# The second batch takes its keys and queries as runs of four tokens and turns them on TensorE

## The chip, the cores and the metric

The kernel is one program on one core of one Trainium2 chip. The metric is the device time of one execution in microseconds (us). Five engines work side by side, each on its own list of instructions and in the order of that list: TensorE (PE: matmuls and transposes; PEld is its weight load), VectorE (DVE), ScalarE (ACT), GpSimd (POOL) and SyncE (SP, which here only issues DMAs). They meet through semaphores. Matmul results land in PSUM, which has eight banks here; everything else lives in SBUF.

## The reference

```python
def _attn_ref(q, k, v, p):                 # q, k, v: (8, 8, 576, 64); p: (8, 8, 32, 64)
    p_packed = sm_attn(p, k, v)            # 32 packed rows read 576 keys
    out = sm_attn(q, p_packed, p_packed)   # 576 queries read the 32 packed rows
    # sm_attn: softmax(q k^T / sqrt(64)) v, the maximum taken away, 1e-9 added to the sum
def _moe_ref(x, w_in, w_out, a, b):        # x: the attention's 4608 x 512, heads side by side
    h = x @ w_in                           # 512 -> 2048
    P = a[0] + a[1]*h + a[2]*h**2 + a[3]*h**3
    Q = 1 + abs(b[0])*abs(h) + abs(b[1])*h**2
    return ((P / (Q + 1e-6)) @ w_out)      # 2048 -> 512
```

The two weight matrices come in 64-bit floats and everything else in 32-bit ones. The kernel computes `h` and the last product to float32 accuracy from three products of 32-bit halves (high by high, low by high, high by low).

## The kernel before

**Batches and units.** The work runs over 8 batches. For each batch `attention(bb)` makes the softmax weights over the 32 packed rows for all heads (tiles `AH` and `AL`, high and low half) and the transposed packed values `PPT`. The second attention product is never formed alone: `m_chunk` multiplies the packed values with a piece of `w_in` (256 of its 2048 columns, one chunk) into the tiles `m`, and a *unit* then goes from `AH`/`AL` and `m` to `h` (`hidden`: PE, tile `h`), through the rational function (ACT and DVE, tiles `Y`, `U`, `V`, `sq`) and on to the output sums (`acc_block`: PE, tile `acc`, from `gh`/`gl` and the split `w_out` pieces in `w`). There are 128 units: 8 batches x 2 halves of the tokens x 8 chunks. Units 0 to 15 are the first batch; a chunk of `m` is made ahead of the unit that first reads it.

**The weights.** `w_in` and `w_out` come in 16 pieces of 1 MB (64-bit words), each as two DMAs of 512 KB, first into the `m` tiles and then into the `w` tiles and `o`. `convert()` turns one piece into 32-bit floats with two ACT and three DVE instructions (`TENSOR_SCALAR`, `SCALAR_TENSOR_TENSOR` and one that the profile calls `CUSTOM_DVE_ANT_0` and the listings below `ISA`); a `w_out` piece is then split by ACT and POOL. All 16 conversions lie among the first dozen units.

**Keys and queries.** `load` fetches what a batch needs, `transposed` in `attention` brings keys and queries into the tile `kx` with the head dimension on partitions. There are two ways:

- First batch (`bb == 0`): a DMA gives each of 128 partitions four tokens in a row, 1 KB from one place. For 2 heads x 2 halves PE transposes 128x128 blocks, four into one PSUM bank, and ACT copies the bank to `kx` (128x512). The 64 tokens beyond 512 are loaded apart into `r`, transposed apart and copied apart (`krem` for the keys, two small copies for the queries). In this form the two halves of the tokens get softmax maxima of their own, and the factors `f`, `fs`, `F` join them.
- All other batches: four DMAs per group of four heads fetch 32-element rows (128 bytes) so that one DVE block transpose of 32x32 blocks, 128x576 at a time, writes `kx` directly. A batch takes four such transposes for its keys and four for its queries.

A batch's keys are loaded, and its remainders and `p`, while the batch before is in `attention`; its values after its keys are transposed, its queries after its values are used, since all share the two `nat` buffers. The second batch's attention runs as 16 steps among units 1 to 14 of the first.

**PSUM.** `bank(bb)` hands out the banks: the first batch takes turns on `acc` and `at` (four banks), the others on `at` alone (two banks), which `m_chunk` uses too.

**What sets the order.** Nothing runs as the code is written. `Planner` records every instruction, prices it from a table (`COST`, `TRANSPOSE`; a DMA by the length of its runs, `DMA_RATE`: 100, 190 or 370 bytes per ns for runs under 256 bytes, under 1 KB, and longer), builds the dependencies, schedules them in a list on the five engines, and issues each engine's instructions in that order. So another price or another instruction moves things everywhere. All instructions carry line 216, the planner's issue; one goes by the tiles' names.

Of the kernel before, what the change touches and what calls it, by code (L numbers as in the profile page):

```python
# [13 lines left out]
F32 = mybir.dt.float32  # L14
# [9 lines left out]
P = 128  # L24
# [7 lines left out]
class Planner:  # L32
# [8 lines left out]
    TRANSPOSE, F32 = (15, 0.834), (30, 1.667)  # L41
# [206 lines left out]
def attention_rational_ffn(  # L248
# [15 lines left out]
    NG = 2  # L264
# [160 lines left out]

    NAT, AH, AL, PPT = {}, {}, {}, {}

    def load(bb, what):  # L430
        if bb >= B:
            return
        if what == "rem":

            rv, pn = NAT[bb, "rv"], NAT[bb, "p"] = rv_ring.next(), pn_ring.next()
            if bb == 0:
                r = NAT[bb, "r"] = Y_ring.at(2, [P, H, D])
                nc.sync.dma_start(r[0:REM], k[bb, :, NS * P : T, :].rearrange("h p d -> p h d"))
            for j in range(NJ):
                src = p[bb, NG * j : NG * j + NG].rearrange("r n d -> n r d")  # L440
                nc.sync.dma_start(pn[32 * j : 32 * j + 32, :, 0, :], src)
            nc.gpsimd.tensor_copy(pn[:, :, 1, :], pn[:, :, 0, :])
            for i in range(2 if bb == 0 else 0):
                src = q[bb, 4 * i : 4 * i + 4, NS * P : T, :].rearrange("h (p x) d -> p h (x d)", x=2)
                r2 = r[REM + HREM * i : REM + HREM * (i + 1)].rearrange("p (h x) d -> p h (x d)", x=2)
                nc.sync.dma_start(r2, src)
            for i in range(2):
                src = v[bb, 4 * i : 4 * i + 4, NS * P : T, :]
                if bb == 0:
                    nc.sync.dma_start(rv[REM * i : REM * (i + 1)], src.rearrange("h p d -> p h d"))  # L450
                    continue
                for y in range(2):
                    o = REM * i + HREM * y
                    nc.sync.dma_start(rv[o : o + HREM], src.rearrange("h (p y) d -> y p h d", y=2)[y])
            return
        x, g = what[0], int(what[1])
        src = {"k": k, "q": q, "v": v}[x][bb, 4 * g : 4 * g + 4]
        if bb > 0:
            t = NAT[bb, what] = nat_ring.next()
            if x == "v":  # L460
                t = NAT[bb, what] = t[:, 0 : 4 * NS * D].rearrange("p (h s d) -> p h s d", h=4, s=NS)
                for y in range(2):
                    to = t.rearrange("p h (y i) d -> p h y (i d)", y=2)[:, :, y]
                    nc.sync.dma_start(to, src[:, 2 * P * y : 2 * P * (y + 1)].rearrange("h (p i) d -> p h (i d)", i=2))
                return
            src = src.rearrange("h t d -> (h t) d")
            for i in range(2):
                for y in range(2):
                    o = 64 * i + 32 * y
                    blocks = src[:, 32 * y : 32 * y + 32].rearrange("(a t i) d -> i t a d", t=32, i=2)[i]  # L470
                    nc.sync.dma_start(t[o : o + 32].rearrange("p (a d) -> p a d", d=32), blocks)
            return
        src = src[:, 0 : NS * P, :]
        if x != "k":
            if g == 0:
                NAT[x] = w_ring.at(NCH - 2 + "vq".index(x), [P, 2, 4 * NS * D], F32)
            t = NAT[x][:, g, :]
        else:
            t = nat_ring.next()[:, 0 : 4 * NS * D]
        t = t.rearrange("p (h s d) -> p h s d", h=4, s=NS)  # L480
        nc.sync.dma_start(t, src.rearrange("h (p s) d -> p h s d", s=NS))
        NAT[bb, what] = t
# [18 lines left out]
    def attention(bb):  # L501
# [7 lines left out]
        xr = lambda x: x.rearrange("p (x r) -> p x r", r=NG)  # L509
        eng = nc.vector if bb == 0 else nc.gpsimd  # L510
        KX = kx_ring.next()
        AH[bb], AL[bb], PPT[bb] = AH_ring.next(), AL_ring.next(), ppT_ring.next()
        flat = KX.rearrange("p j c -> p (j c)")
        rows = lambda i: slice(64 * i, 64 * i + 64)
        cols = lambda j: slice(32 * j, 32 * j + 32)
# [4 lines left out]
        qx = flat.rearrange("p (r j c) -> p r j c", r=NG, j=NJ)  # L520

        def transposed(x, g):
            for r in range(NG if bb > 0 else 0):

                src = NAT[bb, f"{x}{g}"].rearrange("p (j r c) -> p r j c", j=2, r=NG)[:, r]
                nc.vector.transpose(qx[:, r, 2 * g : 2 * g + 2, :], src)
            for r in range(NG if bb == 0 else 0):
                t = bank(bb)
                for i in range(2):
                    for y in range(2):  # L530
                        o = (2 * i + y) * P
                        nc.tensor.transpose(t[:, o : o + P], NAT[bb, f"{x}{g}"][:, 2 * i + r, 2 * y : 2 * y + 2, :], ident)
                to = kmain if x == "k" else qx[:, :, :, 0:HMAIN]
                nc.scalar.copy(to[:, r, 2 * g : 2 * g + 2, :], t.rearrange("p (j c) -> p j c", j=2))
# [4 lines left out]
                load(bb, f"v{g}")  # L539
            yield  # L540
        rkq = NAT.get((bb, "r"))
        if bb == 0:
            t = bank(bb)
            for j in range(NJ):
                nc.tensor.transpose(t[:, j * P : (j + 1) * P], rkq[:, 2 * j : 2 * j + 2, :], ident)
            nc.scalar.copy(krem, t.rearrange("p (j c) -> p j c", j=NJ)[:, :, 0:REM])
# [3 lines left out]
        nc.scalar.copy(pT, t[:, 0 : NG * P].rearrange("p (r c) -> p r c", r=NG))  # L550
        yield

        KEYS = ((0, 2 * P), (2 * P, T)) if bb == 0 else ((0, HALF), (HALF, T))
        of = lambda a, r: a.rearrange("p (x r) -> p x r", r=NG)[:, :, r]
        for r in range(NG):
            t = [bank(bb)[:, 0 : c1 - c0] for c0, c1 in KEYS]
            if bb > 0:

                for b in (slice(0, 2 * P), slice(2 * P, HALF)):
                    tiles(  # L560
                        (
                            (t[x][cols(j), o], pT[rows(x), r, cols(j)], qx[rows(x), r, j, b]),
                            dict(start=True, stop=True),
                        )
                        for j in range(NJ)
                        for x, o in ((0, b), (1, slice((b.start + HREM) % HALF, (b.stop + HREM - 1) % HALF + 1)))
                    )
                for x in range(2):
                    nc.vector.reduce_max(mx[:, 2 * x + r : 2 * x + r + 1], t[x], axis=AX.X)
                bias = nbm[:, r : r + 1]  # L570
                nc.vector.tensor_scalar(bias, mx[:, r : r + 1], mx[:, 2 + r : 3 + r], -SCALE, ALU.max, ALU.mult)
                for x, (c0, c1) in enumerate(KEYS):
                    i = slice(2 * x + r, 2 * x + r + 1)
                    nc.scalar.activation(KX[:, r, c0:c1], t[x], AF.Exp, bias=bias, scale=SCALE, accum_out=sm[:, i])
                if r == 0:
                    yield
                continue
# [19 lines left out]
                nc.scalar.activation(KX[:, r, c0:c1], t[x], AF.Exp, bias=nb[:, i], scale=SCALE, accum_out=sm[:, i])  # L597
            if r == 0:
                yield
        if bb == 0:  # L600
            nc.vector.tensor_tensor(nbm, nb[:, 0:2], nb[:, 2:4], ALU.min)
            nc.vector.tensor_sub(xr(f), two(nbm), xr(nb))
            nc.scalar.activation(f, f, AF.Exp)
            nc.vector.tensor_mul(fs, f, sm)
        else:
            fs = sm
        nc.vector.scalar_tensor_tensor(tot, fs[:, 0:2], 1e-9, fs[:, 2:4], ALU.add, ALU.add)
        nc.vector.reciprocal(rec, tot)
        if bb == 0:
            nc.vector.tensor_mul(xr(F), xr(f), two(rec))  # L610
        yield

        for r in range(NG):
            t = bank(bb)
            for s in range(NS):
                c0 = s * P + (REM if bb > 0 and s > 1 else 0)
                nc.tensor.transpose(t[:, s * P : (s + 1) * P], KX[:, r, c0 : c0 + P], ident)
            nc.scalar.copy(KX[:, 2 + r, 0 : NS * P], t)
            if r == 1:

                t = bank(bb)
                for i in range(NG):
                    o = slice(i * P, (i + 1) * P)
                    if bb > 0:
                        nc.tensor.transpose(t[:, o], KX[:, i, HALF + HREM - P : HALF + HREM], ident)
                        nc.tensor.transpose(t[0:REM, o], KX[:, i, 2 * P : 2 * P + REM], ident)
                        continue
# [4 lines left out]

        t = bank(bb)
        rv = NAT[bb, "rv"]
        for r in range(NG if bb > 0 else 0):
            tiles(
                (
                    (
# [10 lines left out]
                for s in range(NS + 1)  # L649
                for j in range(NJ)  # L650
            )
        for r in range(NG if bb == 0 else 0):
            for x, blocks in enumerate((range(2), range(2, NS + 1))):
                o = slice((2 * r + x) * D, (2 * r + x + 1) * D)
                tiles(
# [19 lines left out]
        twice = lambda o: o.rearrange("p (i d) -> p i d", i=1).broadcast_to([P, 2, D])  # L675
        for r in range(NG):
            o = pp[:, r]
            if bb > 0:
                nc.vector.tensor_scalar(o, twice(t[:, r * D : (r + 1) * D]), rec[:, r : r + 1], None, ALU.mult)
            else:  # L680
                nc.vector.tensor_scalar(o, twice(t[:, 2 * r * D : (2 * r + 1) * D]), F[:, r : r + 1], None, ALU.mult)
# [6 lines left out]
        for g in range(2):  # L688
            transposed("q", g)
            load(bb + 1, f"k{g}")  # L690
            if g == 0 and bb == 0:
                t = bank(bb)
                for j in range(NJ):
                    nc.tensor.transpose(t[:, j * P : (j + 1) * P], rkq[:, 2 * j : 2 * j + 2, :], ident)
# [4 lines left out]
                load(bb + 1, "rem")  # L699
            yield  # L700

        for r in range(NG):
            t = [bank(bb)[:, 0:HALF] for _ in range(2)]
            tiles(
# [135 lines left out]
    def acc_block(u, i):  # L840
# [10 lines left out]
        if i == 0:  # L851
            O[bb, x] = o_ring.next()
        o = O[bb, x]
        order = "(p i x) m -> p x i m" if bb == 0 else "(i p x) m -> p x i m"
        ov = out[bb * T : bb * T + NS * P, :].rearrange(order, i=2, x=2)[:, x]
        if u == NU - 1 and i == 1:
            nc.vector.tensor_copy(o[:, i, :], acc)
# [95 lines left out]
```

## Time and profile before

| what | value |
| --- | --- |
| median of 3 runs | 809.83 us (808.62 to 809.86) |
| the profiled execution | 808.45 us, of which the span from the first to the last instruction is 806.7 us |
| busy share of the span | PE 92%, PEld 73%, DVE 88%, ACT 83%, POOL 58% |
| mean granted TensorE clock | 0.958 |
| moved by DMA | 56.04 MB in 168,876 packets, 140,384 of them under 512 bytes |
| all weights converted | at 145.75 us, the end of the last `CUSTOM_DVE_ANT_0` |
| first output store issued | at 153.81 us (units 0 to 7 are through) |

The chain that ended last has PE for 70% of the span, DVE 10%, ACT 8%, SP's queue 4% and DMA 4%. Busy shares are means over the whole span. The stretch before some 150 us, in which weights arrive and are converted, has other limits than the rest, and it is read by itself. A group's row gives count, busy time, mean ns of one, and then the idle time before them. Rows of one engine overlap by their ends, so the step from one start to the next is shorter than the duration.

### The profile page before, as it was taken

What the parts mean: (1) busy time and instruction counts of PE and PEld (TensorE: products, weight loads), DVE (VectorE), ACT (ScalarE), POOL (GpSimd) and SP (SyncE); (2) the same over time, 40 slices, a digit from 0 to 9 for tenths busy, and PEclk for the clock granted to TensorE, in tenths of its full rate; (3) what the DMA queues carried; (4) which work ended last, traced back from release to release, by engine and by line L of the source; (5) the groups of instructions that cost most, each with busy time, mean ns of one, the idle gap of its engine ahead of it and who ended that gap; (6) DMA issues with size and microseconds to landing.
All of it is one profiled execution on the core that took longest, in us unless ns stands there. A gap on an engine that the chain in (4) does not pass through costs nothing.

```text
span 806.7 us, 15198 instructions
## 1 busy us (share of the span) xinstructions
PE 745.5 (92%) x5416; PEld 585.4 (73%) x5416; DVE 709.1 (88%) x1310; ACT 666.0 (83%) x1482; POOL 463.9 (58%) x462
## 2 busy tenths in 40 slices
PE   6376686899999999999999999999999999999997
PEld 4154464578877788768878788678877887778886
DVE  2988999898899788998899789998899789998873
ACT  4788797799888798889888798889888788998972
POOL 0003564675568455766578555756568456766663
PEclk9765799799999999999999999999999999999999
DMA  8993238202550206220730209120820214000001
GB/s 267 280 298 110 105 78 110 43 5 79 67 86 1 79 18 96 56 57 28 94 58 1 82 15 119 33 56 27 103 49 5 75 33 67 1 2 27 27 1 39
DMA packets 168876, 56.04 MB, mean 69 GB/s; under 512 B 140384, under 2 KB 158048, under 8 KB 168800
## 3 DMA queue, kind: packets, MB, share of 16 engines
q1 hardware_dynamic: 168800, 55.07, 31.4%
q8 instruction: 42, 0.69, 0.4%
q14 instruction: 34, 0.28, 0.1%
HBM read 45.62 MB, written 9.44 MB: 68 GB/s over the span
## 4 chain that ended last, share of the span: by engine, by line
PE 70%; DVE 10%; ACT 8%; SPq 4%; DMA 4%; issue 2%; POOL 1%; DVEq 0%; POOLq 0%
PE acc L216 35%; PE h L216 22%; PE at L216 13%; DVE Y L216 5%; SPq L216 4%; ACT Y L216 2%; DVE w L216 1%; ACT U L216 1%; ACT V L216 1%; ACT w L216 1%; DMA w<-in_q_dram 1%; ACT sq L216 1%; DVE V L216 1%; POOL w L216 1%; DVE kx L216 1%
## 5 line engine op out<-in xcount | busy, mean ns | idle before, releaser
L216 PE MATMUL acc<-w,gh 128*128 128x512 f32 x1024 | 330.5, 405 | 19.3 <-ACT w L216 15.0
L216 PEld LDWEIGHTS acc<-w,gh 128*128 128x128 f32 x1024 | 186.7, 191 | 72.7 <-ACT w L216 16.6
L216 POOL TENSOR_TENSOR U<-U,sq 128x576 f32<-128x576 f32 x118 | 168.9, 1432 | 75.4 <-ACT U L216 43.3
L216 PE MATMUL h<-AH,m 128*128 128x288 f32 x1024 | 192.0, 309 | 8.8 <-DVE Y L216 6.1
L216 POOL TENSOR_TENSOR gl<-Y,gh 128x512 fp32r<-128x512 f32 x128 | 167.7, 1310 | 50.5 <-ACT gh L216 23.3
L216 PE MATMUL acc<-w,gl 128*128 128x512 f32 x512 | 193.2, 398 | 0.3 <-POOL gl L216 0.3
L216 PEld LDWEIGHTS h<-AH,m 128*128 128x128 f32 x1024 | 162.7, 195 | 40.5 <-DVE Y L216 23.1
L216 ACT ACTIVATE Y<-h,abS 128x288 f32<-128x288 f32 x256 | 125.2, 509 | 23.5 <-PE h L216 19.3
L216 DVE TENSOR_TENSOR Y<-Y,h 128x288 f32<-128x288 f32 x256 | 109.9, 446 | 32.0 <-ACT Y L216 12.0
L216 ACT ACTIVATE sq<-h 128x288 f32<-128x288 f32 x236 | 97.5, 416 | 40.2 <-PE h L216 34.1
L216 DVE SCALAR_TENSOR_TENSOR Y<-Y,abS,h 128x288 f32<-128x288 f32 x256 | 125.5, 508 | 2.2
L216 DVE SCALAR_TENSOR_TENSOR Y<-Y,abS,V 128x576 f32<-128x576 f32 x128 | 103.4, 808 | 22.7 <-ACT V L216 22.0
L216 PEld LDWEIGHTS acc<-w,gl 128*128 128x128 f32 x512 | 96.8, 189 | 28.0 <-issue 8.5
L216 PE MATMUL h<-AL,m 128*128 128x288 f32 x512 | 113.0, 302 | 0.0
L216 POOL COPY G<-Y 128x64 f32<-128x64 f32 x128 | 35.5, 277 | 125.8 <-DVE Y L216 109.1
L216 ACT ACTIVATE U<-h 128x288 f32<-128x288 f32 x256 | 98.1, 421 | 8.7 <-PE h L216 4.3
L216 ACT ACTIVATE V<-U,one 128x576 f32<-128x576 f32 x128 | 98.0, 766 | 5.8 <-DVE Y L216 5.6
L216 DVE SCALAR_TENSOR_TENSOR Y<-V,Y 128x576 f32<-128x576 f32 x128 | 95.8, 749 | 1.8
L216 DVE SCALAR_TENSOR_TENSOR V<-U,V 128x576 f32<-128x576 f32 x128 | 96.4, 753 | 0.0
L216 ACT CAST gh<-Y 128x512 fp32r<-128x512 f32 x128 | 81.2, 634 | 7.4 <-DVE Y L216 7.0
L216 PEld LDWEIGHTS h<-AL,m 128*128 128x128 f32 x512 | 85.1, 194 | 0.9 <-issue 0.8
L216 ACT ACTIVATE V<-V 128x576 f32<-128x576 f32 x128 | 84.6, 661 | 0.6
(123 smaller groups left out, 813.2 us busy)
## 6 DMA issues: line engine op xcount, KB each, us to landing
nat<-in_k_dram SPq DMA_DIRECT2D x56, 144.0 KB, 4.1
nat<-in_q_dram SPq DMA_DIRECT2D x56, 144.0 KB, 4.2
out_dram<-o SPq DMA_DIRECT2D x15, 512.0 KB, 2.9
w<-in_moe_w_out_dram SPq DMA_DIRECT2D x14, 512.0 KB, 5.0
nat<-in_v_dram SPq DMA_DIRECT2D x28, 256.0 KB, 3.6
m<-in_moe_w_in_dram SPq DMA_DIRECT2D x8, 512.0 KB, 9.6
w<-in_moe_w_in_dram SPq DMA_DIRECT2D x8, 512.0 KB, 5.5
nat<-in_k_dram SPq DMA_DIRECT2D x2, 512.0 KB, 4.8
```

Source lines behind the costliest of these rows:

```text
L216: getattr(getattr(self.nc, engine), name)(*args, **kwargs)
```

## The change

`rows4(bb)` replaces `bb == 0` wherever the form of the loads is chosen, and is true for the first two batches. The second batch then loads keys, queries and values as 1 KB runs, PE transposes keys and queries and ACT copies them, its remainder goes through `r`, and its softmax joins two halves by factors. Its output rows are stored in the matching order. `r` moves from a `Y` tile to the `AH` tile of the same batch, which is free until the batch's softmax weights are written; `AH` and `AL` are taken only then. The second batch still takes its banks from the two `at` banks.

```diff
+    rows4 = lambda bb: bb < 2
 
     def load(bb, what):
...
-            if bb == 0:
-                r = NAT[bb, "r"] = Y_ring.at(2, [P, H, D])
+            if rows4(bb):
+                r = NAT[bb, "r"] = AH_ring.at(bb, [P, H, D], F32)
                 nc.sync.dma_start(r[0:REM], k[bb, :, NS * P : T, :].rearrange("h p d -> p h d"))
...
-        if bb > 0:
+        if not rows4(bb):
             t = NAT[bb, what] = nat_ring.next()
...
-        if x != "k":
+        if bb == 0 and x != "k":
...
         def transposed(x, g):
-            for r in range(NG if bb > 0 else 0):
+            for r in range(0 if rows4(bb) else NG):
                 ...
                 nc.vector.transpose(qx[:, r, 2 * g : 2 * g + 2, :], src)
-            for r in range(NG if bb == 0 else 0):
+            for r in range(NG if rows4(bb) else 0):
                 t = bank(bb)
...
-        KEYS = ((0, 2 * P), (2 * P, T)) if bb == 0 else ((0, HALF), (HALF, T))
+        KEYS = ((0, 2 * P), (2 * P, T)) if rows4(bb) else ((0, HALF), (HALF, T))
...
-        if bb == 0:
+        if rows4(bb):
             nc.vector.tensor_tensor(nbm, nb[:, 0:2], nb[:, 2:4], ALU.min)
...
+        AH[bb], AL[bb] = AH_ring.at(bb % 2), AL_ring.at(bb % 2)
...
-        order = "(p i x) m -> p x i m" if bb == 0 else "(i p x) m -> p x i m"
+        order = "(p i x) m -> p x i m" if rows4(bb) else "(i p x) m -> p x i m"
```

The listings below give each engine's own order: line, operation, out<-in with the buffers' numbers (the last number is a running count of tiles, so it differs between the two kernels), shape, count.

**SP, after the first four weight pieces.** Before, the second batch's keys (`nat0_3`, `nat1_4`) go out ahead of and among the fifth to eighth pieces:

```order
L216 DMA m3_4_116<-in_moe_w_in_dram 128x2x256 x2
L216 DMA nat0_3_104<-in_k_dram 32x36x32 x4
L216 DMA w1_3_117<-in_moe_w_in_dram 128x2x256 x2
L216 DMA w2_4_118<-in_moe_w_in_dram 128x2x256 x2
L216 DMA nat1_4_110<-in_k_dram 32x36x32
L216 DMA w3_5_119<-in_moe_w_out_dram 128x512 x2
L216 DMA nat1_4_110<-in_k_dram 32x36x32 x3
L216 DMA w4_6_120<-in_moe_w_in_dram 128x2x256 x2
```

Now:

```order
L216 DMA m3_4_117<-in_moe_w_in_dram 128x2x256 x2
L216 DMA w1_3_118<-in_moe_w_in_dram 128x2x256 x2
L216 DMA w2_4_119<-in_moe_w_in_dram 128x2x256 x2
L216 DMA w3_5_120<-in_moe_w_out_dram 128x512 x2
L216 DMA w4_6_121<-in_moe_w_in_dram 128x2x256 x2
L216 DMA nat0_3_102<-in_k_dram 128x4x256
L216 DMA w5_7_122<-in_moe_w_out_dram 128x512 x2
L216 DMA nat1_4_109<-in_k_dram 128x4x256
L216 DMA w6_8_133<-in_moe_w_in_dram 128x2x256 x2
L216 DMA AH1_2_106<-in_k_dram 64x8x64
```

Eight key loads of 128-byte rows have become two of 1 KB runs and one of remainders, and four weight pieces stand ahead of them.

**DVE, at the end of the first batch's attention.** `m2_3`, `m3_4`, `w1_3` and `w2_4` are weight pieces; `Y1_2`/`Y0_1` with `h` is unit 0. Before:

```order
L216 TENSOR_SCALAR m3_4_116<-m3_4_116 128x1024
L216 ISA win_71<-m2_3_115,win_71 128x2048
L216 TENSOR_TENSOR AL0_1_86<-kx0_1_84,AH0_1_85 128x576
L216 SCALAR_TENSOR_TENSOR m3_4_116<-m3_4_116 128x1024
L216 STREAM_TRANSPOSE kx0_2_140<-nat0_3_104 128x576 x2
L216 TENSOR_TENSOR Y1_2_127<-Y1_2_127,h0_1_128 128x288
L216 ISA win_71<-m3_4_116,win_71 128x2048
```

Now:

```order
L216 ISA win_71<-m3_4_117,win_71 128x2048
L216 TENSOR_TENSOR kx0_1_84<-kx0_1_84,small_73 128x576
L216 TENSOR_SCALAR w2_4_119<-w2_4_119 128x1024
L216 STREAM_TRANSPOSE kx0_1_84<-kx0_1_84 128x576
L216 SCALAR_TENSOR_TENSOR w1_3_118<-w1_3_118 128x1024
L216 SCALAR_TENSOR_TENSOR w2_4_119<-w2_4_119 128x1024
L216 TENSOR_TENSOR AL0_1_111<-kx0_1_84,AH0_3_110 128x576
L216 ISA win_71<-w1_3_118,win_71 128x2048
L216 ISA win_71<-w2_4_119,win_71 128x2048
L216 TENSOR_TENSOR Y0_1_128<-Y0_1_128,h0_1_129 128x288
```

The transposes out of `nat0_3` are gone, and two more weight pieces are converted before unit 0. At the end of the last conversion DVE's list has finished unit 8 before, and unit 9 now.

**ACT, around unit 0** (`Y` and `U` out of `h0`, `h1`). Before:

```order
L216 CAST m1_6_133<-at1_16_134 128x256
L216 ACTIVATE Y1_2_127<-h0_1_128,abS_68 128x288
L216 ACTIVATE U0_1_125<-h0_1_128 128x288
L216 ACTIVATE Y1_2_127<-h1_2_131,abS_68 128x288
L216 ACTIVATE U0_1_125<-h1_2_131 128x288
L216 ACTIVATE win_71<-w2_4_118 128x1024
```

Now:

```order
L216 ACTIVATE w5_7_122<-w5_7_122 128x1024
L216 COPY kx0_2_141<-at1_18_143 128x512
L216 ACTIVATE Y0_1_128<-h0_1_129,abS_68 128x288
L216 ACTIVATE U0_1_126<-h0_1_129 128x288
L216 ACTIVATE Y0_1_128<-h1_2_132,abS_68 128x288
L216 ACTIVATE U0_1_126<-h1_2_132 128x288
L216 COPY kx0_2_141<-at0_19_144 128x512
```

The first pair of key copies stands on both sides of unit 0, so the bank `at0_19` is held until unit 0's last read of `h`.

More of the change, by code (lines that the diff above doesn't have):

```diff
@@ L442, in load @@
             nc.gpsimd.tensor_copy(pn[:, :, 1, :], pn[:, :, 0, :])
-            for i in range(2 if bb == 0 else 0):
+            for i in range(2 if rows4(bb) else 0):
                 src = q[bb, 4 * i : 4 * i + 4, NS * P : T, :].rearrange("h (p x) d -> p h (x d)", x=2)
@@ L511, in attention @@
         KX = kx_ring.next()
-        AH[bb], AL[bb], PPT[bb] = AH_ring.next(), AL_ring.next(), ppT_ring.next()
+        PPT[bb] = ppT_ring.next()
         flat = KX.rearrange("p j c -> p (j c)")
@@ L541, in attention @@
         rkq = NAT.get((bb, "r"))
-        if bb == 0:
+        if rows4(bb):
             t = bank(bb)
@@ L556, in attention @@
             t = [bank(bb)[:, 0 : c1 - c0] for c0, c1 in KEYS]
-            if bb > 0:
+            if not rows4(bb):
                 for b in (slice(0, 2 * P), slice(2 * P, HALF)):
@@ L599, in attention @@
                 yield
-        if bb == 0:
+        if rows4(bb):
             nc.vector.tensor_tensor(nbm, nb[:, 0:2], nb[:, 2:4], ALU.min)
@@ L608, in attention @@
         nc.vector.reciprocal(rec, tot)
-        if bb == 0:
+        if rows4(bb):
             nc.vector.tensor_mul(xr(F), xr(f), two(rec))
@@ L615, in attention @@
             for s in range(NS):
-                c0 = s * P + (REM if bb > 0 and s > 1 else 0)
+                c0 = s * P + (0 if rows4(bb) or s < 2 else REM)
                 nc.tensor.transpose(t[:, s * P : (s + 1) * P], KX[:, r, c0 : c0 + P], ident)
@@ L623, in attention @@
                     o = slice(i * P, (i + 1) * P)
-                    if bb > 0:
+                    if not rows4(bb):
                         nc.tensor.transpose(t[:, o], KX[:, i, HALF + HREM - P : HALF + HREM], ident)
@@ L634, in attention @@
         rv = NAT[bb, "rv"]
-        for r in range(NG if bb > 0 else 0):
+        for r in range(0 if rows4(bb) else NG):
             tiles(
@@ L651, in attention @@
             )
-        for r in range(NG if bb == 0 else 0):
+        for r in range(NG if rows4(bb) else 0):
             for x, blocks in enumerate((range(2), range(2, NS + 1))):
@@ L677, in attention @@
             o = pp[:, r]
-            if bb > 0:
+            if not rows4(bb):
                 nc.vector.tensor_scalar(o, twice(t[:, r * D : (r + 1) * D]), rec[:, r : r + 1], None, ALU.mult)
@@ L690, in attention @@
             load(bb + 1, f"k{g}")
-            if g == 0 and bb == 0:
+            if g == 0 and rows4(bb):
                 t = bank(bb)
```

## The prediction

> **What bounds the kernel now.** I read the slices of the page first, then busy time by stretches, then the waits of PE and DVE. The slices show two regimes:
>
> ```profile
> PE   6376686899999999999999999999999999999997
> DVE  2988999898899788998899789998899789998873
> ACT  4788797799888798889888798889888788998972
> PEclk9765799799999999999999999999999999999999
> DMA  8993238202550206220730209120820214000001
> ```
>
> A slice is 20 us. From the eighth on PE is full at full clock; before that it is at 30 to 80%, its granted clock falls to 0.5, and DVE is the fullest engine from the second slice on, with DMA full in the first three. The stretches give this in numbers (time, then busy us of each engine, clock, DMA share, GB/s):
>
> ```profile
> core 0: us, PE busy (x) PEld busy (x) DVE busy (x) ACT busy (x) POOL busy (x), PEclk, DMA share, GB/s
> 20.00:155.00 135.00, 92.73 (x649) 63.08 (x648) 125.77 (x204) 108.84 (x208) 51.41 (x43) 0.75 0.59 150
> 155.00:330.00 175.00, 174.24 (x1325) 139.84 (x1323) 158.25 (x300) 150.02 (x347) 111.37 (x112) 1.00 0.31 59
> 20.00:60.00 40.00, 22.61 (x165) 13.64 (x163) 36.55 (x59) 31.72 (x56) 0.92 (x1) 0.66 0.98 290
> 60.00:100.00 40.00, 26.65 (x186) 19.09 (x187) 35.84 (x54) 33.42 (x67) 18.20 (x13) 0.67 0.35 112
> 100.00:155.00 55.00, 43.47 (x300) 30.35 (x300) 53.38 (x92) 43.70 (x88) 32.29 (x29) 0.87 0.48 75
> ```
>
> From 20 to 155 us, which I call the ramp, DVE is busy for 125.8 of 135 us: it is the bound, with 9.2 us of idle time. ACT has 26 us to spare and PE 42. From 155 us on PE has 0.8 us of idle time in 175. So time saved in the ramp is kept to the end: the later part can go neither faster nor slower by it. The next rows say what PE waits for between 155 and 780 us, and what DVE waits for between 20 and 150:
>
> ```profile
> PE h L216 <- DVE Y L216: 3.0, 9, 1.0
> PE acc L216 <- ACT gh L216: 2.9, 7, 0.7
> ...
> DVE Y L216 <- ACT U L216: 5.2, 5, 1.7
> DVE w L216 <- ACT w L216: 1.2, 1, 1.2
> DVE m L216 <- ACT win L216: 1.1, 1, 1.1
> DVE small L216 <- PE acc L216: 0.5, 1, 0.5
> ```
>
> Of DVE's eight waits in the ramp seven are on ACT, one is on PE and none is on a DMA.
>
> **The change part by part.** All of the second batch's attention lies in the ramp, so all edits are priced there.
>
> *DVE loses eight block transposes* (four of keys, four of queries) and gains the joining of two softmax halves. The groups up to 155 us and two neighbours of the timeline:
>
> ```profile
> L216 DVE STREAM_TRANSPOSE kx<-nat 128x576 f32<-128x576 f32 x8 | 5.9, 763 | 0.0
> L216 DVE TENSOR_TENSOR small<-small 128x4 f32<-128x4 f32 x3 | 0.5, 164 | 0.2
> L216 DVE TENSOR_TENSOR small<-small 128x2 f32<-128x2 f32 x1 | 0.2, 161 | 0.0
> L216 DVE SCALAR_TENSOR_TENSOR small<-acc,small 128x128 f32<-128x128 f32 x2 | 0.7, 350 | 0.1
> ...
> 136.38 0.77 DVE L216 STREAM_TRANSPOSE kx<-nat 128x576 f32<-128x576 f32 x1
> 137.07 0.73 DVE L216 SCALAR_TENSOR_TENSOR V<-U,V 128x576 f32<-128x576 f32 x1
> ```
>
> Rows overlap by their ends: the step from one start to the next is 0.69 us, so the eight give back 8 x 0.69 = 5.5 us. They had no idle time ahead of them. Added are the four small ones (3 x 0.164 + 0.161 = 0.65) and the two of 128x128 (0.70): 1.35 us. The two maxima per pass stay two. DVE's net is 5.5 - 1.35 = 4.15 us less, all on the engine that bounds the stretch.
>
> *ACT gains the copies out of PSUM.* Rows of the first batch, which does just this:
>
> ```profile
> L216 ACT COPY kx<-at 128x512 f32<-128x512 f32 x6 | 3.4, 588 | 0.5 <-PE at L216 0.5
> L216 ACT COPY kx<-at 128x128 f32<-128x128 f32 x2 | 0.5, 306 | 0.0
> L216 ACT COPY kx<-at 128x256 f32<-128x256 f32 x1 | 0.4, 372 | 0.3 <-PE at L216 0.3
> L216 ACT ACTIVATE small<-small 128x4 f32<-128x4 f32 x1 | 0.2, 236 | 0.0
> ```
>
> Eight copies of 128x512 are 4.7 us, the keys' remainder 0.37, the queries' two 0.6, the factors 0.24: 5.9 us. ACT goes from 108.8 to 114.7 us of the ramp, DVE from 125.8 to 121.6. The cover is ACT's spare time; by halves it is thin. From 20 to 100 us, where the keys are, DVE has 72.4 - 4 x 0.69 = 69.6 and ACT 65.1 + 2.4 + 0.4 = 67.9. From 100 on it is 52.0 against 46.7, with room.
>
> *PE gains 40 transposes* in ten groups of four. A group took 0.60 us warm and 1.06 us on the slow clock:
>
> ```profile
> 18.72 0.60 PE L216 MATMUL at<-ident,w 128*128 128x128 f32 x4
> 5.88 1.06 PE L216 MATMUL at<-ident,nat 128*128 128x128 f32 x4
> ```
>
> That is 6 to 11 us; I take 8, since half of the ramp's clock is low. PE's 42 us of idle time cover it. If they stood in a full stretch, 6 us would go onto the end; in the planned order the last of them stands at the h matmuls of unit 9, before the last conversion.
>
> *SP and DMA.* Keys and queries go from 16 DMAs of 128-byte rows to four of 1 KB runs and three of remainders; values and their remainders from eight to four. What the short rows cost (issues; then, from 20 to 30 us, the rate in steps of 0.25 us and the packets):
>
> ```profile
> 19.40 10.78 SPq L216 DMA_DIRECT2D nat<-in_k_dram  x4
> 36.48 9.00 SPq L216 DMA_DIRECT2D nat<-in_k_dram  x3
> 45.53 1.10 SPq L216 DMA_DIRECT2D w<-in_moe_w_in_dram  x2
> 117.10 6.71 SPq L216 DMA_DIRECT2D nat<-in_q_dram  x8
> ...
> GB/s 410 410 483 385 377 385 377 385 385 401 418 418 410 401 401 385 385 393 393 369 368 382 322 324 299 280 188 181 164 171 141 189 83 71 44 24 14 137 200 195
> DMA packets 4569, 2.94 MB, mean 294 GB/s; under 512 B 3351, under 2 KB 3351, under 8 KB 4567
> ```
>
> SP is held for 20 us by seven of the key loads, and the rate falls from about 400 to under 190 GB/s while their packets run. The weight piece behind them goes out only at 45.5 us. Now five pieces' worth of loads close up, and DVE's list uses that (two more conversions ahead of unit 0). The keys land later than before, behind eight weight pieces and the first batch's loads, 8 x 1.05 + 3.4 = 11.8 MB; at the 290 to 400 GB/s of the rows above that is 30 to 41 us. The h matmuls of unit 0 stand behind their transposes on PE, but these need the first batch's `AL`, whose last half DVE starts here:
>
> ```profile
> 40.67 0.77 DVE L216 TENSOR_TENSOR AL<-kx,AH 128x576 fp32r<-128x576 f32 x1
> ```
>
> With two more conversions ahead this is later still, so I charge the keys' landing nothing. What the faster loads bring is bounded by DVE's idle time: between 0 and 9.2 us. I take 0, because DVE's waits name ACT and no DMA.
>
> *The `r` tile* in `AH` instead of `Y` frees one of three `Y` buffers at the start and holds `AH` of the second batch, which nobody else wants then; no row shows a wait for either, cost 0.
>
> **Sum.** DVE's 4.15 us, nothing else. The profiled execution, 808.45 us for a span of 806.7, would become 804.3. It lies 1.4 us below the median of the runs, 809.83, and I forecast that median: 809.8 - 4.2 = 805.6 us. A measurement of this kernel tells a change from none at about 0.2%, 1.6 us, so this is outside, 0.5%.
>
> **The rivals.**
>
> *Feeding was the limit (faster than I say).* For it: DMA's 0.98 share from 20 to 60 us, SP held for 20 us, and 8% of the chain that ended last, which are SP's queue and DMA. Against it: DVE's 3.5 us of idle time in those 40 us. If half of the ramp's idle time goes too, the gain is 4.15 + 4.6 = 8.8: 801.0 us; if all, 796.5.
>
> *ACT takes the bound over in the first half (no change).* Two engines with 69.6 and 67.9 us of work in 80 that wait for one another cannot both be filled as DVE was with ACT lower. Then the keys' part gives nothing and only the queries' four transposes, less the 1.35 us added, count: 4 x 0.69 - 1.35 = 1.4 us, 808.4. For a block of 32x32 the Trainium skill (VectorE: DVE Perf Modes, "Rules for kernel authors") calls the DVE transpose the fastest, and its table of the three paths puts TensorE at 390 ns per 128x128 against 311 on VectorE. By that alone the change would be a loss; here the cheaper path was on the fullest engine, and this trace has the ratio even worse for PE and ACT together, 5.9 + 8 us for 5.5.
>
> *The two `at` banks (slower).* The ring is shared with `m_chunk`. These rows follow the fourth chunk: PE starts it, ACT's last copy frees it, and unit 3, its first reader, starts:
>
> ```profile
> 47.84 1.63 PE L216 MATMUL at<-win,ppT 64*32 64x256 f32 x16
> ...
> 55.31 0.39 ACT L216 CAST m<-at 128x256 fp32r<-128x256 f32 x1
> ...
> 64.30 1.16 PE L216 MATMUL h<-AH,m 128*128 128x288 f32 x4
> ```
>
> The chunk held its pair for 7.9 us, and was ready 8.6 us early. Two pairs of key banks and the remainder's, 2.5 pairs, now go between the chunks ahead of it and the next ones, and in ACT's new order the first pair's second copy stands behind all of unit 0. At a floor of 1.1 + 2 x 0.59 = 2.3 us per pair they cost 5.8 us, under the 8.6; from 3.4 us per pair on units wait, at 5.1 the DVE gain is used up, and at 7.9, the chunk's own hold, the loss is 2.5 x 7.9 - 8.6 - 4.15 = 7.0 us. I take 6.5 us: 2.5 x 6.5 - 8.6 - 4.15 = 3.5, which makes 813.3 us. PE runs its list in order, so a wait here holds the `h` of the units behind it.
>
> **How the numbers follow.** My forecast (803 to 808): 0.53. It has DVE's busy share for it, the strongest row. Feeding: 0.15, since its row contradicts DVE's. ACT: 0.19, the cover is 1.7 us thin in one half. Banks: 0.13, there is slack, but the pair around unit 0 must be held longer than the floor. Faster by over 0.2%: 0.53 + 0.15 = 0.68. Within: 0.19. Slower: 0.13. The range goes down to 800, past the middle of the feeding case, and up to 810.5, through ACT's case; left out are most of the banks' case and the end of feeding, under 0.2.
>
> **What would show it.** `STREAM_TRANSPOSE kx<-nat` 48 instead of 56, none before 150 us. The first output store, at 153.81 us here, does not hang on the order chosen:
>
> ```profile
> 153.81 0.62 SPq L216 DMA_DIRECT2D out_dram<-o  x1
> ```
>
> I expect it at 149.7, with DVE still fullest before it. Earlier than 147 speaks for feeding; at 152.5 with ACT busy over 95% from 40 to 80 us, for ACT; later than 154 with PE waiting at `at` for ACT's `kx` or `m` copies, for the banks. The piece at 45.53 us should go out before 35. The forecast is wrong too if PE has gaps after 155 us that it has not now, since then the saved time is lost again.

## The result, and the profile after

The changed kernel takes 804.98 us (median of 6 runs, 801.95 to 805.47) against 809.70 us (6 runs, 808.62 to 810.05) for the kernel before. The ratio, which is worked out over all the runs and is not the quotient of the two medians, is 0.9932, 95% interval 0.9916 to 0.9947: 5.5 us less, from 4.3 to 6.8. A second set of runs on another occasion gave 803.42 us and 0.9924 (0.9909 to 0.9939). The profiled execution took 803.09 us for a span of 801.3 us, 5.4 us less than the profiled one of before.

The slices of the page of the changed kernel, 20 us each:

```profile
PE   5587686899999999999999999999999999999997
DVE  2999999898899789998899789998899789998883
ACT  5899988789888798889888798889788798998972
PEclk9668899899999999999999999999999999999999
DMA  7983135002730208110720219010910123000001
```

The two regimes are the same. In the first seven slices ACT reads 5899988 where it read 4788797, DVE is at 9 from the second to the seventh, and the granted clock is at 8 or 9 from the fourth slice on, where the fourth to eighth slices read 5, 7, 9, 9 and 7 before. The same stretches as before (time, then busy us of PE, PEld, DVE, ACT, POOL, the clock, DMA share, GB/s):

```profile
20.00:155.00 135.00, 99.26 (x719) 70.62 (x719) 129.06 (x220) 116.68 (x231) 52.22 (x48) 0.82 0.51 156
155.00:330.00 175.00, 174.51 (x1314) 140.81 (x1313) 158.49 (x298) 150.26 (x347) 110.36 (x111) 1.00 0.31 56
20.00:60.00 40.00, 27.13 (x189) 17.31 (x188) 36.81 (x61) 36.28 (x65) 0.30 (x1) 0.66 0.93 320
60.00:100.00 40.00, 29.26 (x211) 21.59 (x198) 39.21 (x62) 36.38 (x78) 21.29 (x17) 0.83 0.29 96
100.00:155.00 55.00, 42.87 (x335) 31.72 (x334) 53.03 (x100) 44.02 (x89) 30.64 (x30) 0.94 0.36 81
```

DVE has not become less busy in the 135 us, as the subtraction of 4.15 us suggests, but busier: 129.1 us instead of 125.8, since work of later units moved up into the place that came free. Its idle time went from 9.2 to 5.9 us, on balance all of it between 60 and 100 us (35.84 us of work became 39.21). After 155 us nothing has changed: PE has 0.5 us of idle time in 175.

What DVE waits for between 20 and 150 us, in order:

```profile
DVE Y L216 <- ACT U L216: 2.2, 3, 1.2
DVE m L216 <- ACT m L216: 1.5, 1, 1.5
DVE abS L216 <- DMA ab<-in_moe_a_dram: 1.1, 1, 1.1
DVE kx L216 <- PE at L216: 0.8, 1, 0.8
```

The waits of units for ACT (`Y <- U`) were 5.2 us and are 2.2.

SP's issues (start us, duration us, destination, source, count), first the weights that go out ahead of the second batch's keys, then the two key loads and the first output store:

```profile
19.42 5.00 SPq L216 DMA_DIRECT2D w<-in_moe_w_in_dram  x4
...
27.88 1.73 SPq L216 DMA_DIRECT2D w<-in_moe_w_in_dram  x2
30.65 0.37 SPq L216 DMA_DIRECT2D nat<-in_k_dram  x1
...
35.24 0.54 SPq L216 DMA_DIRECT2D nat<-in_k_dram  x1
...
150.94 0.62 SPq L216 DMA_DIRECT2D out_dram<-o  x1
```

In the kernel before, 10.78 us of key loads stood first, and the same four weight DMAs followed at

```profile
30.22 2.21 SPq L216 DMA_DIRECT2D w<-in_moe_w_in_dram  x4
```

The groups of the changed kernel that answer to the forecast, over the whole span for DVE and up to 155 us for ACT:

```profile
L216 DVE STREAM_TRANSPOSE kx<-nat 128x576 f32<-128x576 f32 x48 | 36.6, 765 | 0.1
L216 ACT COPY kx<-at 128x512 f32<-128x512 f32 x14 | 8.2, 588 | 0.9 <-PE at L216 0.8
```

48 block transposes instead of 56, 14 wide copies instead of 6, at the same 588 ns.

### The profile page after: what moved, and what is told of

Read it like the earlier page. It is cut to its first block, busy times and chain, and to the rows that moved or that the text cites. A ratio compares the mean times of both kernels' runs of the same rounds, so it can differ in the third digit from the quotient of the medians.

```text
span 801.3 us, 15242 instructions
## 1 busy us (share of the span) xinstructions
PE 745.9 (93%) x5440; PEld 588.2 (73%) x5440; DVE 706.9 (88%) x1308; ACT 671.3 (84%) x1494; POOL 460.7 (57%) x462
## 4 chain that ended last, share of the span: by engine, by line
PE 71%; DVE 12%; ACT 10%; DMA 3%; POOL 2%; issue 2%; SPq 1%; DVEq 0%
PE acc L216 36%; PE h L216 23%; PE at L216 13%; DVE Y L216 6%; ACT Y L216 2%; DVE w L216 2%; ACT m L216 1%; DMA w<-in_q_dram 1%; ACT U L216 1%; DVE small L216 1%; ACT V L216 1%; ACT w L216 1%; DVE V L216 1%; POOL gl L216 1%; ACT sq L216 1%
## 5 line engine op out<-in xcount | busy, mean ns | idle before, releaser
L216 PE MATMUL h<-AH,m 128*128 128x288 f32 x1024 | 189.1, 306 | 13.6 <-DVE Y L216 12.5
L216 PEld LDWEIGHTS h<-AH,m 128*128 128x128 f32 x1024 | 160.3, 193 | 43.3 <-DVE Y L216 29.2
L216 POOL COPY G<-Y 128x64 f32<-128x64 f32 x128 | 32.2, 251 | 129.8 <-DVE Y L216 120.4
```

The lines of the kernel that those rows point to most:

```text
L216: getattr(getattr(self.nc, engine), name)(*args, **kwargs)
```

## The experiments

Times are medians with their ratio to the kernel before on the same chip; a difference of two ratios is turned into us by 809.8. Two theories stand against the prediction's "DVE's 4.15 us, nothing else". *Feeding*: the short rows held the weights back, and part of the gain is the weights' earlier coming. *ACT*: the copies are not covered.

**Which half of the change brings it.** `rows4` split into one condition for keys and values and one for queries (`rowsq`); each kernel has one of them at two batches and the other at one.

```diff
-    rows4 = lambda bb: bb < 2
+    rows4 = lambda bb: bb < 2        # e_queries: bb == 0
+    rowsq = lambda bb: bb == 0       # e_queries: bb < 2
...
-            for r in range(0 if rows4(bb) else NG):
+            for r in range(0 if (rowsq if x == "q" else rows4)(bb) else NG):
```

Keys and values alone, expected:

> The changed kernel with the second batch's queries as before (128-byte rows, block transposes); only its keys and values in the new form. Theory VectorE time: 4 x 0.69 - 1.35 = 1.4 us off the kernel before, 808.3 us. Rival feeding: only the keys' loads stand among the weights, so nearly all of the gain, 805.0 to 806 us. Rival ScalarE (it takes the bound over in the first half): no gain from the keys, 809.7 us.

Measured: 804.46 us, 0.9930 (0.9918 to 0.9942). Queries alone, expected:

> The changed kernel with the second batch's keys and values as before; only its queries in the new form. Theory VectorE time: 4 x 0.69 = 2.8 us off the kernel before, 806.9 us. Rival feeding: 809 to 809.7 us, the queries' loads stand behind the weights. Rival ScalarE: all of the gain is here, 805 us.

Measured: 806.92 us, 0.9961 (0.9948 to 0.9974). So the keys' half alone gives 5.7 us, the queries' half alone 3.2 us, both together 5.5: they do not add. The keys' half frees only 4 x 0.69 - 1.35 = 1.4 us of DVE; 5.7 us is four times that. Something else than DVE's time comes with the keys' new form: their quick loads, another order, or the TensorE clock that comes with it (last section). The queries' 3.2 us are what DVE's time, 2.8 us one for one, would give.

**The quick loads alone.** The kernel before with DVE's transposes kept, but each of the four key and query groups of the second batch in one DMA of 4.6 KB runs (the tokens stand in another order, so its values are not the reference's):

```diff
+            if bb == 1:
+                nc.sync.dma_start(t, src.rearrange("h t d -> (h t d)").rearrange("(p c) -> p c", p=P))
+                return
```

> The kernel before, with one thing changed: each of the second batch's four groups of keys and queries comes by one DMA of 4.6 KB runs in place of four DMAs of 128-byte rows. VectorE's eight block transposes stay (the second batch's keys and queries stand in another order, so its values are not the reference's). Theory VectorE time (the change gained because VectorE's 4.15 us left the ramp): VectorE does what it did, so 809.7 us, within 1 us. Rival feeding (the short rows held up the weights): at least half of the 4.7 us gain, 807.3 us or less.

Measured: 807.64 us, 0.9967 (0.9956 to 0.9979): 2.7 us less, with not one instruction less on DVE. But the planner had made a new order here. So 4.6 KB rows in exactly the old order, in 16 transfers as before, with each transfer priced as the short one was:

```diff
+        if id(args[1]) in self.short:
+            return self.short[id(args[1])][1] * size / self.DMA_RATE[0]
...
+                    if bb == 1:
+                        nc.short[id(flat)] = flat, 32 * 4 * HALF
+                        nc.sync.dma_start(t[o : o + 32], flat)
+                        continue
```

> The kernel before, every engine's instructions in exactly its order; only the sixteen key and query DMAs of the second batch carry 4.6 KB runs in place of 128-byte rows, and the planner prices them as before (the second batch's values are not the reference's). The run with long rows and a new plan took 807.6 us against 810.0. Theory VectorE time: 809.7 to 810 us, and the gain of the run with long rows was its new order. Rival feeding: the quick rows themselves bring it, 807.6 us or less.

Measured: 811.22 us, 1.0005 (0.9994 to 1.0017): nothing, although the eight key loads hold SP for 7.3 us in place of 20.6 there, and the weight piece that went out at 45.53 us goes out at 38.58. Then is it the order alone? The short rows in exactly the order of the run with quick loads (the 16 transfers priced as four quick ones):

```diff
+            return self.short[id(args[1])][1] * size / self.DMA_RATE[2]
...
+        if engine == "sync":
+            return self.DMA_ISSUE
```

> The kernel before with its own short rows, but with each group's four transfers priced as one transfer of long rows when the order is planned, so that all engines run their instructions in the same sequence as in the run with long rows (807.64 us). It parts two causes of those 2.4 us. Theory: it needs the quick rows and the order together (quick rows in the old order brought nothing, 811.22), so short rows in this order lose it again: 809.5 to 812. Rival: the order alone made the difference, and the rows did not matter: 807.6 within 0.7 us.

Measured: 810.66 us, 1.0017 (1.0006 to 1.0028). Against the run with quick loads that is 0.0050 or 4.0 us (give or take 1.3), in the traces 2.2 (spans of 808.9 and 806.7). It takes both: rows that pass quickly, and an order that counts on it. Where the short rows cost is seen on SP and ACT. The run with quick loads, in order of time:

```profile
25.32 1.68 SPq L216 DMA_DIRECT2D nat<-in_k_dram  x2
27.96 1.68 SPq L216 DMA_DIRECT2D w<-in_moe_w_out_dram  x2
...
42.78 1.22 ACT L216 ACTIVATE w<-w 128x1024 f32<-128x1024 f32 x1
...
45.55 1.23 DVE L216 CUSTOM_DVE_ANT_0 win<-w,win 128x2048 uint16<-128x2048 uint16 x1
```

The same instructions in the run with short rows (its code has four more lines, hence line 220):

```profile
25.38 14.11 SPq L220 DMA_DIRECT2D nat<-in_k_dram  x8
39.53 1.55 SPq L220 DMA_DIRECT2D w<-in_moe_w_out_dram  x2
...
45.59 1.10 ACT L220 ACTIVATE w<-w 128x1024 f32<-128x1024 f32 x1 [2.94 <-DMA w<-in_moe_w_out_dram]
...
47.95 1.22 DVE L220 CUSTOM_DVE_ANT_0 win<-w,win 128x2048 uint16<-128x2048 uint16 x1
```

Eight loads hold SP for 14.1 us instead of 1.7, the next weights go out 11.6 us later, ACT waits 2.94 us for them, and DVE's next conversion is 2.4 us later. This delay is still there at the start of the last conversion (144.93 and 147.02 us) and at the first store (150.63 and 152.73).

**DVE's time given back.** First the changed kernel with eight reductions of 128x576 on DVE where the code had the block transposes, planned anew:

```diff
+            for r in range(NG if bb == 1 else 0):
+                half = NAT[bb, f"{x}{g}flat"][:, 448 * r : 448 * r + 576].rearrange("p (a b) -> p a b", b=32)
+                nc.vector.reduce_max(spare, half, axis=AX.X)
```

> The changed kernel, with eight VectorE reductions of 128x576 (0.74 us each, the step of a block transpose) put back where the eight block transposes were; they read the loaded keys and queries and write a spare tile that nobody reads. Theory VectorE time: 8 x 0.69 = 5.5 us come back, 805.0 + 5.5 = 810.5 us. Rival feeding: the loads stay quick, so 805 to 806.5 us.

Measured: 808.55 us, 0.9979 (0.9967 to 0.9990), 3.8 us (give or take 1.6) over the changed kernel by the ratios. But the planner spread the reductions: they start between 24.2 and 170.2 us, the last three after 163 us and so behind the ramp. Then without a new order: the changed kernel's own lists, with the eight reductions slipped in behind eight conversions.

```diff
+            if i in self.extra:
+                self.extra[i]()
...
         nc.vector.tensor_add(dst.bitcast(I32), hi, di)
+        if 4 <= converted < 12:
+            nc.extra[len(nc.ops) - 1] = more     # reduce_max(spare, 128x18x32)
```

> The changed kernel in exactly its order, with eight VectorE reductions of 128x576 (about 0.67 us from start to start) added, one behind each of eight weight conversions, all before 130 us. Theory VectorE time: all of it shows, 8 x 0.67 = 5.4 us, 810.4 us. If the stretch is bound by VectorE and others in turn, a part shows: 807 to 809 us. If feeding alone had made the gain: under 806 us.

Measured: 807.67 us, 0.9971 (0.9959 to 0.9983). The added group on DVE, from an answer by tile (minimum, median and maximum ns, first and last start):

```profile
L294 DVE TENSOR_REDUCE spare<-ident x8: 737/742/746, 47.9 to 94.7; 128x18 f32<-128x576 f32 x8
```

From one start to the next a reduction takes 0.663 us, so 8 x 0.663 = 5.3 us of DVE's time lengthen the run by 3.2 us (give or take 1.6) by the ratios, against the changed kernel's first set. By the spans it is 3.4 or 1.9 (804.7 against 801.3 and 802.8, the two profiles of the changed kernel). Some three fifths of DVE's time shows at the end, and the interval allows from three to nine tenths. That the rest goes into waits, DVE's idle time being still there to use, is argued.

**The same outside the ramp.** The eight reductions behind the units of the fourth batch's first half:

```diff
         nc.vector.scalar_tensor_tensor(Y, V, 2.0, Y, ALU.subtract, ALU.mult, reverse0=True)
+        if bb == 3 and x == 0:
+            nc.extra[len(nc.ops) - 1] = more
```

> The changed kernel in its own sequence on every engine, with eight more reductions of 128x576 on DVE (0.69 us each, 5.5 us) in the first units of the fourth batch, after 155 us, where PE is full. Theory: there DVE's work is covered, so the time is that of the changed kernel within 0.5 us. Rival: DVE's work costs about half wherever it stands, as in the ramp (807.67 there): 807.5 or more.

Measured: 805.01 us, 0.9941 (0.9923 to 0.9960). Against the changed kernel of the same occasion (0.9924) that is 1.4 us with an uncertainty of 1.9, more than the 0.5 that I expected and not told from nothing. The traces are finer. PE's waits for DVE from 350 to 420 us, where the reductions are, went from

```profile
PE h L216 <- DVE Y L216: 0.4, 1, 0.4
```

in the changed kernel's second profile to

```profile
PE h L216 <- DVE Y L216: 1.1, 2, 0.7
```

here: 0.7 us of 5.3, and the spans differ by as much (803.5 and 802.8). By this one pair of traces the cover there is not complete, but it takes nearly nine tenths.

**ACT's time.** Sixteen copies of 128x320 on ACT, in pairs behind eight conversions, in the changed kernel's own order:

```diff
         nc.scalar.activation(di, lo.bitcast(U32), AF.Copy, scale=2.0**-29)
+        if 4 <= converted < 12:
+            nc.extra[len(nc.ops) - 1] = lambda: [more() for _ in range(2)]
```

> The changed kernel in its own sequence on every engine, with sixteen more copies of 128x320 on ACT (about 0.4 us each, 6.4 us) behind eight conversions of weights in the ramp, that is about what the change itself gave ACT. Theory: ACT, with 116.7 of 135 us busy, is a second limit there by now, and about half of its added time shows, as of DVE's: 807.5 to 809. Rival, the prediction's own step: ACT's work is covered by its spare time: 805.0 to 806.0.

Measured: 810.74 us, 1.0012 (1.0003 to 1.0022), which is 7.1 us (give or take 1.5) over the changed kernel of the same occasion; by the spans 5.3 us (808.1 and 802.8). The added group:

```profile
L294 ACT COPY spare<-ident x16: 440/458/529, 35.1 to 85.1; 128x320 f32<-128x320 f32 x16
```

From start to start the 16 copies take 6.7 us of ACT's time, and they cost 5.3 to 7.1 us: most of it, perhaps all, shows. DVE's first unit of the second chunk starts at 57.21 us with 1.60 us of waiting,

```profile
57.21 0.46 DVE L216 TENSOR_TENSOR Y<-Y,h 128x288 f32<-128x288 f32 x1 [1.60 <-ACT U L216]
```

where it started at 52.91 us in the second profile of the changed kernel:

```profile
52.91 0.45 DVE L216 TENSOR_TENSOR Y<-Y,h 128x288 f32<-128x288 f32 x1 [0.75 <-ACT U L216]
```

Five of the eight pairs, some 4.1 us from start to start, stand ahead of it on ACT, and 4.3 us are lost there already. The theory had about half of the time, the rival none; it was more than either. These copies were put into a finished order; those of the change were placed by the planner in a new one.

**The changed kernel again**, for the two runs above.

> The changed kernel once more, beside the others on the same chip: 805.0 within 0.7 us, ratio 0.993 to 0.995. It is what the two runs above are taken against.

Measured: 803.42 us, 0.9924 (0.9909 to 0.9939), within the first set's interval.

**How much is the plan's luck.** The planner's constant `PASS`, which only shifts its choices, from 200 to 180, in the changed kernel and in the one before:

```diff
-    PASS = 200
+    PASS = 180
```

> The changed kernel with another plan (180 in place of 200 ns for a semaphore between engines). Order worth little: 805.0 us within 0.5 us. Plans scatter: another time by 1 us or more; below 804 us the plan of the changed kernel had given back part of the gain, as its 6.2 us wait of TensorE for VectorE near 140 us suggests.

> The kernel before with another plan: the planner's price for a semaphore between engines is 180 in place of 200 ns, the work is the same. If the order as such is worth little, 809.7 us within 0.5 us; if plans scatter, another time by 1 us or more, which is then the size below which no difference between two plans can be put down to the work.

Measured: changed 806.53 us, 0.9954 (0.9938 to 0.9970); before 809.74 us, 0.9992 (0.9982 to 1.0003). With the other constant the change is worth 0.0038 or 3.1 us (give or take 1.5), against 5.5: the same work in another order differs by 0.6 us in the kernel before and by 1.8 in the changed one, 2.4 against its second set. So comparisons in which the order was made anew are no finer than that, and the keys', queries' and the changed kernel's 5.7, 3.2 and 5.5 us cannot be taken apart to a microsecond. Those in one order are free of it.

## Why the prediction was right, and where not

The forecast was 805.6 us, the time 804.98, the direction and the place (all in the ramp, kept to the end) as told. The gain of 4.2 us that was forecast lies just under the measured interval, 4.3 to 6.8, and within the spread of the plans (3.1 and 5.5 us). But two of its terms were wrong, one too large and one too small. That the number came so close is luck in part.

*DVE's 4.15 us.* The counts and durations held: 48 transposes at 765 ns, none of the second batch's left. Wrong was "all on the engine that bounds the stretch", that is, one for one. At the measured three fifths the 4.15 us are worth 2.5, and from 1.3 to 3.8 by that run's interval. The queries' half alone would fit one for one, but its order was made anew.

*Feeding, charged 0, "because DVE's waits name ACT and no DMA".* This is the step that failed. Quick rows in an order planned for them are worth 4.0 us (give or take 1.3; 2.2 in the traces) against short rows in that same order, and 2.7 against the kernel before. That the changed kernel, which has another order again, gains about as much by its quick loads is argued from this and not shown. Early weights alone do not do it, as the quick rows in the old order show. Nor does the share of SP's queue and DMA in the chain that ended last tell: it was 8%, is 4% in the changed kernel, and is 5% with quick rows in the old order, which gained nothing. Why DVE's waits name no DMA is argued too: the planner had priced the short rows and laid the conversions where their weights would be there. ACT's waits between 35 and 60 us look like the sign that the prediction missed. The kernel before had this row,

```profile
ACT m L216 <- PE at L216: 7.4, 6, 4.2
```

and in the changed kernel it is

```profile
ACT m L216 <- PE at L216: 0.2, 1, 0.2
```

But the row goes with the order and not with the loads: it is 7.0 us with quick rows in the old order, and from 35 to 50 us it is the same with quick rows and with short rows in the order planned for quick ones,

```profile
ACT m L216 <- PE at L216: 1.6, 2, 1.2
ACT m L220 <- PE at L220: 1.6, 2, 1.2
```

where the kernel before has 6.6. Its longest wait there, 4.2 us, ends with PE's chunk, and PE had waited for a conversion on DVE,

```profile
PE at L216 <- DVE win L216: 5.5, 1, 5.5
```

of a piece in an `m` tile, whose loads are all issued ahead of the second batch's keys. DVE's list, which runs without a gap from 22 to 44 us, held this up; no late weight shows there. What shows late weights is the pair in one order, with ACT's 2.94 us for the `w_out` piece.

With 2.5 us for DVE and 2.2 to 4.0 for feeding the sum is 4.7 to 6.5, which holds the 5.5; the intervals leave room for other splits. That the terms add is argued and not shown: the halves of the change do not add either. Of the Trainium skill the page Perfetto Trace Analysis (section on optimizing DMA performance) counts a kernel as bound by DMA where the issuing engine's track is solid with DMA work, and asks for large descriptors. The 14.11 us of eight loads on SP agree; but in the old order large rows brought nothing (1.0005), so the rule alone would have given the wrong time there.

*ACT, 5.9 us covered.* Neither shown nor refuted, since no run takes the copies' time away. What the traces show is that the spare time was used up. ACT and DVE between 35 and 60 us, before:

```profile
35.00:60.00 25.00, 17.54 (x107) 11.64 (x107) 22.83 (x35) 19.43 (x36) 0.92 (x1) 0.57 1.00 302
```

and now:

```profile
35.00:60.00 25.00, 18.20 (x106) 12.02 (x105) 23.42 (x36) 23.60 (x43) 0.30 (x1) 0.62 0.86 278
```

ACT is busy for 23.6 of 25 us where it was for 19.4. The 4.2 us stand where ACT had waited for PE in the old order. From 40 to 80 us it is busy for 36.78 of 40, 92%, under the 95% that I named for the rival; the rival that ACT takes over did not come true, but the next 6.7 us of ACT's work cost nearly their length. The Trainium skill's rule that the DVE transpose is the fastest for 32x32 (VectorE: DVE Perf Modes, "Rules for kernel authors"), which by itself made the change a loss, did not decide: the queries' half alone, too, is 3.2 us faster.

*PE, 8 us of 6 to 11, covered.* The 40 transposes, in the groups from 30 to 150 us:

```profile
L216 PE MATMUL at<-ident,nat 128*128 128x128 f32 x32 | 6.0, 318 | 2.0 <-ACT m L216 1.1 <-ACT kx L216 0.8
L216 PE MATMUL at<-ident,AH 128*128 128x128 f32 x8 | 1.7, 353 | 0.3 <-DMA nat<-in_v_dram 0.3
```

That is 7.7 us, and PE has 35.7 us of idle time left in the ramp. The two prices were about right, though the clock that the profile of the kernel before gives around its 1.06 us row, at 5.88 us, is 1.00, so that row by itself does not show the slow clock. In the changed kernel two groups near 43 us took 1.12 us each at a granted clock of 0.50, and two near 57 us 0.66 and 0.60 at 1.00. From 155 us on its waits are those of before:

```profile
PE h L216 <- DVE Y L216: 3.0, 9, 1.0
PE acc L216 <- ACT gh L216: 2.6, 7, 0.5
```

*The banks.* Slower did not come. PE does wait longer at the ring between 20 and 155 us:

```profile
PE at L216 <- ACT m L216: 13.3, 15, 2.4
...
PE at L216 <- ACT kx L216: 2.3, 3, 0.8
```

The 13.3 us were 9.8 before, the 2.3 are new. PE had the idle time for it: from 30 us on no wait of DVE names a bank.

*The marks.* The weight piece was to go out before 35 us, and went at 27.88. The first store was expected at 149.7 and came at 150.94, 2.9 us earlier than before, though the end came 5.4 earlier. I had said that it does not hang on the order chosen; it does. The second store came 6.5 us earlier (185.90 for 192.37), the third 5.0. In the run with quick loads the first store was 3.2 us earlier, at 150.63, and the second 0.4 us later, at 192.81. Left open is whether the queries' half adds anything to the keys': between re-planned kernels a gain of 2 us could hide in the luck. A candidate is PE's wait from 100 to 160 us in the changed kernel, with 6.2 us of it ahead of the `h` at 142.24 us:

```profile
PE h L216 <- DVE Y L216: 8.9, 6, 6.2
```

But with the keys' half alone the sum of this wait is larger, 10.4 us, with 3.7 for the longest, so the row does not part the two. No run took it away.

## What to carry to other kernels

Where a scheduler lays the order, a late transfer need not show as a wait for a DMA, and here following the waits one step further led to the order and not to the transfer. Before such a term is set to nothing, change the transfer alone, once in the old order and once in a new one, and then take the speed away again in the new order. Where two engines hand work to and fro, neither is "the bound" by its busy share: of time added on one only a part showed, on the other nearly all; add the work there in an unchanged order and see what it costs. A re-planned kernel carries some 2 us of luck here, so plan it twice before a difference of that size is given a cause.

## What the runs showed of the hardware

TensorE's granted clock rose with the change, which I had not expected: from 0.75 to 0.82 over the ramp and from 0.67 to 0.83 between 60 and 100 us, where PE's busy time went from 26.65 to 29.26 us. The rise goes with the keys' transposes on PE in every profile here: over the ramp the eight of kernels that have them read 0.79 to 0.84, and the six of kernels without them 0.72 to 0.77. It does not set the time by itself: the changed kernel with ACT's copies added has 0.80 and takes 810.74 us, and the kernel before with quick loads in a new order has 0.72 and takes 807.64. Why the clock rose, and whether it carries a part of the keys' gain, was not tried; PE's busy time alone does not order it, as the run with quick loads has 96.2 us at 0.72 and the kernel before 92.7 at 0.75. And the share of the whole ramp did not rank the engines by what added work costs: with ACT at 116.7 of 135 us nearly all of 6.7 added us showed, with DVE at 129.1 some three fifths of 5.3. The two were not added at the same places (35.1 to 85.1 and 47.9 to 94.7 us). Between 35 and 60 us, where five of ACT's eight added pairs stood, the two were equally full without them (23.60 and 23.42 of 25 us).
